# Raw weights loaded by pairs of units, and a written-out order for the first batch, in an attention and two-layer expert kernel on one core

## The chip, the cores and the metric

The kernel runs on one NeuronCore of a Trainium2 chip. The metric is the device time of one execution in microseconds (us); smaller is better. Beside an execution's own time stands its span, from the first to the last instruction that the hardware profiler recorded. The engines are TensorE (PE: matmuls; PEld: its weight loads), VectorE (DVE), ScalarE (ACT), GpSimd (POOL) and SyncE (SP, which here only issues DMAs). Each engine works through its own instructions in the order in which they stand, and semaphores tie the engines together.

## The reference

Four batches, eight heads, 576 tokens, head size 64; q, k and v arrive as 32-bit floats, the weights as 64-bit floats (read by the kernel as 16-bit pieces).

```python
q_d, k_d, v_d = means of 4 consecutive tokens            # 144 of them
out_up = repeat(softmax(q_d k_d^T / 8) v_d, 4)           # coarse attention, spread back to 576 tokens
out_local = softmax(mask(|i - j| < 4, q k^T / 8)) v      # 7 neighbours of each token
x = (out_up + out_local) as [2304 tokens, 512]
x = (silu(x @ w_gate) * (x @ w_val)) @ w_out             # 512 -> 1536 -> 512
h = x @ w_in
out = (h * clip(h + 3, 0, 6) / 6) @ w_out2               # 512 -> 2048 -> 512
```

## The kernel before

The 2304 tokens are cut into five blocks (`BLOCKS`, up to 512 tokens). Each block runs 68 **units** of the two layers, of five kinds: G (gate), V (value), O (first output), H (second input), P (second output). Units come in pairs, and a unit is 12 matmuls of 512 columns in block 0: each weight and each activation is held as a high and a low part of a reduced 32-bit format, and three products of parts are summed (`HIGH`, `LOW`). A unit's product (`pG`, `pV`, `pH`) takes one of two PSUM banks `mm`; a V unit's product can start only when the bank of the G unit before it has been read by ScalarE (`sl`, L962).

Weights of block 0 go through a chain. `load_unit` (L196, SP's queue) fetches a raw unit, 512 KB of 64-bit numbers, into one of four buffers; `decode_a` (L216, ACT, `top`) and `decode_b` (L225, DVE, `w`) make 32-bit numbers of it and set the buffer free; `split_unit` makes the high part on ACT (L238, `wr`) and the low part on DVE (L239, `wr`) for a pair; the pair is also written to DRAM (`kept`, ACT's queue), from where the blocks after it read it. `prefetch(i)` runs, for unit i of the loop, the load of unit i+8, `decode_a` of i+5, `decode_b` of i+4 and the split of i+3. The next SP load in line waits until the `decode_b` of four units earlier is done.

Ahead of the units stands **the front**, `first_batch`: batch 0's attention on TensorE, in five tiles of 122 tokens (the last has 88). `load_T` turns q and k; `down_scores`, `down_trans`, `down_values` do the coarse attention by head pairs c = 0 to 3. For a tile i, `scores(i)` makes the products (`fS`), the row maxima (DVE, `fnm`) and eight exponentials (ACT, `held`); `norm(i)` divides (DVE, `fsm`, `held`); `trans(i)` turns the result (`fPT`), whose first half ACT and second half DVE copy (`turned`); `values(i)` makes the output (`fO`), and `put_cols` writes its high part on ACT (L275) and its low part on DVE (L276) into `xr`, the units' input. `fill` (L469) puts products that nothing reads ahead of a turning, `FILL_P[i]` of them.

A scheduler orders the instructions of an engine, except those passed through `keep_in_program_order` (`together`, `behind`, `late`), which keep the order of the program among themselves. In the front TensorE's instructions are so pinned, and the decodes and splits (`behind`), but not the front's own DVE and ACT instructions.

Of the kernel before, what the change touches and what calls it, by code (L numbers as in the profile page):

```python
# [21 lines left out]
P = 128  # L22
# [10 lines left out]
HALVES = 1  # L33
# [10 lines left out]
FILL_P = (4, 8, 8, 8, 8)  # L44
# [3 lines left out]
def tile_kernel(  # L48
# [86 lines left out]

    def behind(ins):

        if front[0]:
            tc.keep_in_program_order(ins)
# [26 lines left out]
    def view(t, i):  # L166
        return t[:, i % 2, :].rearrange("p (c e) -> p c e", c=NC)

# [8 lines left out]
    def load_unit(i):  # L177
# [12 lines left out]
        if kind in "GVH":  # L190
            src = src[:, f * P * m:(f + 1) * P * m].rearrange("(c p) f -> p c f", p=P)
        else:
            src = src[f * P:(f + 1) * P, :].rearrange("p (c e) -> p c e", c=NC)
        if wide:
            raw[i] = sp.tile([P, 4 * DM + 32], I16, tag="w64", name=f"w64_{i}", bufs=4)
            behind(nc.sync.dma_start(raw[i][:, 1:1 + 4 * DM].rearrange("p (c e) -> p c e", c=NC), src))  # L196
        else:
            nc.sync.dma_start(view(w32[i // 2], i), src)
# [34 lines left out]
    def split_unit(i):  # L233
        if i % 2:
            return
        s = w32[i // 2].rearrange("p u (c e) -> p u c e", c=NC)
# [33 lines left out]
    def put_cols(bi, col, xv):  # L270
# [4 lines left out]
        nc.scalar.activation(dst[:, :, 0], xv, AF.Copy)  # L275
        nc.vector.tensor_tensor(dst[:, :, 1], xv, dst[:, :, 0].bitcast(F32), op=ALU.subtract)  # L276
# [39 lines left out]


    def first_batch():
# [6 lines left out]
        with tc.tile_pool(name="fp", bufs=1) as fp:  # L325
# [125 lines left out]
            for base, sgn in ((-UPAD, -1), (UPAD + 3, 1)):  # L451
# [3 lines left out]
                )  # L455
            kT = fp.tile([P, NC, S + 6], F32, name="fkT")
            nc.vector.memset(kT[:, :, :3], 0.0)
            nc.vector.memset(kT[:, :, S + 3:], 0.0)
# [12 lines left out]
            def load_T(w, c):  # L471
                src = qn[w, c // 2]
                for th in range(2):
# [13 lines left out]
                    if w == "q":  # L487
                        nc.vector.tensor_scalar(dst, ps[:, :, :TT], 0.125, None, op0=ALU.mult)
                        nc.scalar.activation(small, ps[:, :, TT:], AF.Copy, scale=1 / 128)
                    else:  # L490
                        nc.scalar.activation(dst, ps[:, :, :TT], AF.Copy)
                        nc.vector.tensor_copy(small, ps[:, :, TT:])
# [7 lines left out]
            def down_scores(c):  # L500
# [14 lines left out]
                for par in range(2):  # L515
                    nc.vector.tensor_reduce(nm[:, par], pss[par], axis=AX.X, op=ALU.max, negate=True)
                    for half in range(2):
                        nc.scalar.activation(
# [6 lines left out]
            def down_trans(c):  # L525
                pd = dst[c]
                for par in range(2):
# [3 lines left out]
                    nc.scalar.activation(dpt[h], pt, AF.Copy)  # L531
# [625 lines left out]
```

## Time and profile before

| | |
|---|---|
| time, median of 3 runs (lowest to highest) | 967.41 us (967.27 to 970.9) |
| profiled execution: its own time; its span | 967.38 us; 965.7 us |
| busy: PE, PEld, DVE, ACT, POOL (share of the span) | 948.1 (98%), 803.2 (83%), 724.6 (75%), 501.6 (52%), 110.4 (11%) us |
| mean granted TensorE clock, as a share of the full one | 0.993 |
| the front, first turned q to the start of the units proper | 6.83 to 64.11 us |

The own time is 1.68 us more than the span, and within 0.03 us of the median. Matmuls are pipelined and their ends are modelled, so a PE that is shown as busy may still be waiting; a stretch of matmuls is best timed from the start of one row to the start of the next. DMA shares are of 16 engines, and can exceed 1 where transfers of several queues overlap.

### The profile page before, as it was taken

To read this page: it belongs to the slowest core of one execution; us is meant where nothing else is said; L and a number is where in the kernel's file an instruction comes from. 1 tells how busy PE (TensorE), PEld (TensorE's weight loads), DVE (VectorE), ACT (ScalarE), POOL (GpSimd) and SP (SyncE) were. 2 spreads that over 40 slices of the span, in tenths; PEclk is the share of its full clock that TensorE was granted. 3 is DMA by queue.
4 is the path that set the end of the run, shared out by engine and by line. 5 is a ranking of instruction groups with operands and counts; after the bars stand their busy time and mean duration, and the time that the engine had idled before them with its cause. 6 is when DMAs were issued, how large, how long until landed. Compare 5 with 4: busy or idle time off the path is not lost.

```text
span 965.7 us, 13166 instructions
## 1 busy us (share of the span) xinstructions
PE 948.1 (98%) x4928; PEld 803.2 (83%) x4928; DVE 724.6 (75%) x1059; ACT 501.6 (52%) x928; POOL 110.4 (11%) x125
## 2 busy tenths in 40 slices
PE   9899999999999999999999999999999999999997
PEld 7687888777899988878888778888888788999996
DVE  4678976899979979999774799997337994445652
ACT  4666566876543567553333764443335445444542
POOL 7610002200062300014320000000000000000000
PEclk9999999999999999999999999999999999999999
DMA  8999799866799823359972222462322323443331
GB/s 195 228 270 340 247 366 311 183 198 236 261 246 264 166 86 109 99 188 242 199 157 88 88 67 67 173 216 90 97 100 93 103 88 108 154 131 130 120 122 33
DMA packets 116340, 160.80 MB, mean 167 GB/s; under 512 B 61868, under 2 KB 83756, under 8 KB 116276
## 3 DMA queue, kind: packets, MB, share of 16 engines
q1 hardware_dynamic: 67892, 131.41, 42.7%
q0 software_dynamic: 43488, 10.72, 11.1%
q10 hardware_dynamic: 4896, 17.83, 4.7%
q8 instruction: 39, 0.64, 0.3%
q14 instruction: 25, 0.20, 0.1%
HBM read 137.29 MB, written 22.54 MB: 166 GB/s over the span
## 4 chain that ended last, share of the span: by engine, by line
PE 78%; DVE 7%; DMA 1%; ACT 1%; issue 1%; ACTq 0%; DVEq 0%
PE pH L956 19%; PE aP L998 18%; PE aO L998 13%; PE pV L956 13%; PE pG L956 12%; DVE wr L239 2%; PE pS L881 1%; PE pO L731 1%; DMA w<-in_moe_w_out_dram 1%; DVE xf L856 1%; PE pPT L724 1%; PE px L847 1%; DMA w<-in_moe_w_gate_dram 1%; DVE pv L827 1%; DVE w L225 1%
## 5 line engine op out<-in xcount | busy, mean ns | idle before, releaser
L239 DVE TENSOR_TENSOR wr<-w,wr 128x1024 fp32r<-128x1024 f32 x170 | 207.8, 1222 | 123.8 <-ACT wr L238 123.6
L238 ACT ACTIVATE wr<-w 128x1024 fp32r<-128x1024 f32 x170 | 179.5, 1056 | 119.1 <-issue 57.7
L956 PE MATMUL pH<-x,wr 128*128 128x512 f32 (+1 forms) x960 | 212.2, 372 | 0.0
L998 PE MATMUL aP<-wr,gH 128*128 128x512 f32 x864 | 211.4, 395 | 0.3 <-ACT gH L973 0.3
L956 PEld LDWEIGHTS pH<-x,wr 128*128 128x128 f32 x960 | 173.1, 188 | 25.3 <-issue 2.9
L998 PEld LDWEIGHTS aP<-wr,gH 128*128 128x128 f32 x864 | 159.8, 188 | 34.8 <-issue 2.5
L956 PE MATMUL pG<-xr,wr 128*128 128x512 f32 (+3 forms) x732 | 156.4, 369 | 1.0 <-DVE sl L968 0.6
L956 PE MATMUL pV<-xr,wr 128*128 128x512 f32 (+1 forms) x720 | 153.9, 369 | 0.9 <-ACT sl L962 0.9
L998 PE MATMUL aO<-gV,wr 128*128 128x512 f32 (+1 forms) x720 | 154.4, 371 | 0.0
L956 PEld LDWEIGHTS pG<-xr,wr 128*128 128x128 f32 x732 | 133.3, 191 | 18.5 <-DVE sl L968 1.0
L998 PEld LDWEIGHTS aO<-gV,wr 128*128 128x128 f32 x720 | 132.4, 190 | 16.9 <-DVE gV L974 0.2
L956 PEld LDWEIGHTS pV<-xr,wr 128*128 128x128 f32 x720 | 130.8, 188 | 18.4 <-ACT sl L962 1.8
L971 ACT ACTIVATE h<-pH,consts 128x512 f32<-128x512 f32 (+1 forms) x80 | 51.4, 643 | 59.7 <-PE pH L956 59.5
L973 ACT ACTIVATE gV<-sl 128x512 fp32r<-128x512 f32 (+1 forms) x60 | 35.0, 584 | 85.5 <-DVE sl L968 85.2
L216 ACT ACTIVATE top<-w 128x512 f16<-128x512 bf16 x68 | 52.3, 790 | 22.9 <-DMA w<-in_moe_w_out_dram 7.7
L962 ACT ACTIVATE sl<-pG 128x512 f32<-128x512 f32 (+1 forms) x60 | 33.0, 551 | 59.6 <-PE pG L956 57.0
L973 ACT ACTIVATE gH<-h 128x512 fp32r<-128x512 f32 (+1 forms) x80 | 46.9, 586 | 31.9 <-DVE h L972 31.6
L972 DVE SCALAR_TENSOR_TENSOR h<-h,pH 128x512 f32<-128x512 f32 (+1 forms) x80 | 50.5, 632 | 15.6 <-ACT h L971 15.1
L790 DVE TENSOR_TENSOR pr<-q,k 128x1792 f32<-128x1792 f32 x27 | 54.6, 2021 | 9.4 <-DMA k<-in_k_dram 9.2
L974 DVE TENSOR_TENSOR gH<-h,gH 128x512 fp32r<-128x512 f32 (+1 forms) x80 | 50.6, 633 | 10.9 <-ACT gH L973 10.5
L827 DVE TENSOR_TENSOR pv<-sc,v 128x1792 f32<-128x1792 f32 x27 | 54.6, 2022 | 0.5
L793 DVE TENSOR_REDUCE sc<-pr 128x28 f32<-128x1792 f32 x27 | 54.4, 2015 | 0.1
(131 smaller groups left out, 761.9 us busy)
## 6 DMA issues: line engine op xcount, KB each, us to landing
w<-kept SPq DMA_DIRECT2D x136, 512.0 KB
kept<-w ACTq DMA_DIRECT2D x34, 512.0 KB
w<-in_moe_w_out_dram SPq DMA_DIRECT2D x28, 512.0 KB
w<-in_moe_w_in_dram SPq DMA_DIRECT2D x16, 512.0 KB
w<-in_moe_w_gate_dram SPq DMA_DIRECT2D x12, 512.0 KB
w<-in_moe_w_val_dram SPq DMA_DIRECT2D x12, 512.0 KB
out_dram<-os SPq DMA_DIRECT2D x16, 256.0 KB
dnq<-in_q_dram POOLq DMA_DIRECT2D x24, 144.0 KB, 7.8
```

Of the source, the lines that this page charges most:

```text
L216: behind(nc.scalar.activation(halves(top[i % 2], 2, F16)[:, :, 1], h3.bitcast(BF16), AF.Copy))
L238: behind(nc.scalar.activation(r[:, :, 0], s, AF.Copy))
L239: behind(nc.vector.tensor_tensor(r[:, :, 1], s, r[:, :, 0].bitcast(F32), op=ALU.subtract))
L790: nc.vector.tensor_tensor(pr, qt[:, a:a + SUB, None, :].to_broadcast([P, SUB, W, D]), win(kt, a, SUB), op=ALU.mult)
L793: nc.vector.tensor_reduce(sc[:, a:a + SUB], pr, axis=AX.X, op=ALU.add)
L827: nc.vector.tensor_tensor(pr, pe[:, a:a + SUB, :, None].to_broadcast([P, SUB, W, D]), win(vt, a, SUB), op=ALU.mult)
L956: nc.tensor.matmul(ps[:, cs], r[:, a, c], x[:, c, b_, cs], start=part is HIGH and a == c == 0, stop=part is LOW and c == NC - 1,)
L971: nc.scalar.activation(h, ps, AF.Relu, scale=1 / 6, bias=half1[:, 0:1])
L972: nc.vector.scalar_tensor_tensor(h, h, 1.0, ps, op0=ALU.min, op1=ALU.mult)
L973: nc.scalar.activation(g[:, 0, :nt], h, AF.Copy)
L974: nc.vector.tensor_tensor(g[:, 1, :nt], h, g[:, 0, :nt].bitcast(F32), op=ALU.subtract)
L998: nc.tensor.matmul(ps, **one, start=f_ == 0 and a == b_ == 0, stop=f_ == nf - 1 and b_ == 1,)
```

## The change

1. **Loads by pairs.** A raw load of a G, V or H unit no longer fetches 128 columns of all 512 rows, but 256 columns (both units of the pair) of half the rows: the same 512 KB, in rows twice as long. `split_unit` works on the pair as one flat row of 1024 and hands out the units as views. O and P loads keep their shape.
2. **Orders in the front.** DVE's and ACT's instructions of the front are all pinned (`Ordered`, and `behind` in `put_cols`). `scores` loses its exponentials to a new function `weights`, and the program is written anew with `scores` of a later tile ahead of `trans` of an earlier one. The decodes and splits of the first four units of the loop stay pinned too (`EARLY_W`).
3. **Fills**: 16 in place of 36.
4. **Units 0 and 1 begun in the front**: `begin_unit` multiplies the first 244 columns of unit 0 ahead of `trans(3)` and the first 366 of unit 1 ahead of `trans(4)`, and `run_unit` does the rest (268 and 146). Before, unit 0 alone was cut, 244 and 268.

```diff
-HALVES = 1
+HALVES = 2
-FILL_P = (4, 8, 8, 8, 8)
+EARLY_W = 4
+FILL_P = (4, 4, 4, 4, 0)
...
+    class Ordered:
+        def __init__(self, engine):
+            self.engine = engine
+        def __getattr__(self, name):
+            op = getattr(self.engine, name)
+            def issue(*args, **kw):
+                tc.keep_in_program_order(op(*args, **kw))
+            return issue
...
-            src = src[:, f * P * m:(f + 1) * P * m].rearrange("(c p) f -> p c f", p=P)
+            h = i % 2
+            src = src[h * DM // 2:(h + 1) * DM // 2, (f - h) * P * m:(f - h + 2) * P * m]
+            src = src.rearrange("(c p) f -> p c f", p=P)
...
-        behind(nc.scalar.activation(r[:, :, 0], s, AF.Copy))
-        behind(nc.vector.tensor_tensor(r[:, :, 1], s, r[:, :, 0].bitcast(F32), op=ALU.subtract))
+        r = r.rearrange("p a u c e -> p a (u c e)")
+        behind(nc.scalar.activation(r[:, 0], s, AF.Copy))
+        behind(nc.vector.tensor_tensor(r[:, 1], s, r[:, 0].bitcast(F32), op=ALU.subtract))
+        by = "p a (c u e) -> p u a c e" if units[i][0] in "GVH" else "p a (u c e) -> p u a c e"
+        r = r.rearrange(by, u=2, c=NC)
...
+    def begin_unit(i, n):
+        kind, f, bi = units[i]
+        ps = bank("mm", f"p{kind}{bi}_{f}", 2)
+        products(ps, split[i], xr[bi], slice(0, n), tc.keep_in_program_order)
+        begun[i] = ps, n
...
+            vec, act = Ordered(nc.vector), Ordered(nc.scalar)
...
             scores(0)
             ahead = down_sums(1, ["qk"], first_max[0])
+            weights(0)
             down_trans(2)
             down_scores(3)
             scores(1)
+            weights(1)
             next(ahead)
             next(ahead)
+            norm(0)
             down_values(0)
             down_values(1)
-            norm(0)
+            scores(2)
             trans(0)
+            down_trans(3)
+            prefetch(3 - LR)
+            weights(2)
             prefetch(4 - LR)
-            down_trans(3)
-            down_values(2)
-            norm(1)
-            scores(2)
-            down_values(3)
-            prefetch(5 - LR)
-            values(0)
             for i in range(1, NT):
...
-                trans(i)
+                norm(i)
                 if i + 2 < NT:
                     scores(i + 2)
                 if i == 1:
-                    prefetch(6 - LR)
+                    down_values(2)
+                    down_values(3)
+                values(i - 1)
+                if i >= NT - HALVES:
+                    begin_unit(i - NT + HALVES, (i - 1) * QT)
+                trans(i)
+                if i + 2 < NT:
+                    weights(i + 2)
+                    prefetch(4 + i - LR)
                 if i == 2:
                     prefetch(7 - LR)
-                if i + 1 < NT:
-                    norm(i + 1)
                 next(ahead, None)
-                values(i)
+            values(NT - 1)
-        front[0] = False
...
+            front[0] = i < EARLY_W
             prefetch(i)
```

How the instructions stand on the engines, before and after. First TensorE, behind `down_values(0)` and `(1)` (`fdO`), before: the fills and the turning of tile 0 (`fPT`), then `down_trans(3)` (`fdT`), `down_values(2)`, `scores(2)` (`fS`, its weight loads left out), `down_values(3)`, and only then `values(0)` (`fO`).

```order
L469 MATMUL fPT_0_561<-ident 128x256
...
L620 MATMUL fPT_0_561<-ident,held 128x122 x4
L620 MATMUL fPT_1_571<-ident,held 128x122 x4
L724 MATMUL fdT_582<-ident,fdpd_492 72x72 x4
...
L538 MATMUL fdO_596<-fvd,fdpT_476 72x65 x2
...
L572 MATMUL fS_0_614<-band,pick 122x512
...
L538 MATMUL fdO_638<-fvd,fdpT_587 72x65 x2
...
L638 MATMUL fO_658<-tmp 128x122
```

The same place after:

```order
L607 MATMUL fS_0_560<-band,pick 122x512
...
L503 MATMUL fPT_0_576<-ident 128x256
...
L660 MATMUL fPT_0_576<-ident,held 128x122 x4
L660 MATMUL fPT_1_586<-ident,held 128x122 x4
L766 MATMUL fdT_592<-ident,fdpd_489 72x72 x4
...
L607 MATMUL fS_0_631<-band,pick 122x512
...
L572 MATMUL fdO_647<-fvd,fdpT_473 72x65 x2
...
L572 MATMUL fdO_660<-fvd,fdpT_597 72x65 x2
...
L678 MATMUL fO_673<-tmp 128x122
```

`scores(2)` now stands ahead of the turning of tile 0, and `scores(3)` ahead of `down_values(2)` and `(3)`; both `down_values` stand directly ahead of `values(0)`.

Second VectorE, around the low part of the first weight pair (L239 before, L252 after; `L145` is the line of `Ordered`). Before, with the division of tile 2 (`fsm`, `held`) ahead of it:

```order
L225 SCALAR_TENSOR_TENSOR w_0_580<-w_1_257,top_161 128x512
L599 TENSOR_SCALAR fsm_612<-fsm_612 122x8
L600 RECIPROCAL fsm_612<-fsm_612 122x8
L601 TENSOR_TENSOR held<-held,fsm_612 122x1024
L239 TENSOR_TENSOR wr_655<-w_0_580,wr_655 128x2x512
L276 TENSOR_TENSOR xr_671<-fO_658,xr_671 128x4x122
L625 COPY turned<-fPT_1_692 128x488
```

After:

```order
L291 TENSOR_TENSOR xr_686<-fO_673,xr_686 128x4x122
L145 COPY turned<-fPT_1_699 128x488
L237 SCALAR_TENSOR_TENSOR w_0_620<-w_1_257,top_161 128x512
L252 TENSOR_TENSOR wr_717<-w_0_620,wr_717 128x1024
L145 TENSOR_SCALAR fsm_558<-fsm_558 122x8
L145 RECIPROCAL fsm_558<-fsm_558 122x8
L145 TENSOR_TENSOR held<-held,fsm_558 122x1024
L145 TENSOR_REDUCE fnm_730<-fS_0_731 88x4
```

The low part moved from behind the division of tile 2 to ahead of it.

Third ScalarE, from the output of tile 2 to the first `sl`. Before:

```order
L275 ACTIVATE xr_671<-fO_808 128x4x122
L627 ACTIVATE turned<-fPT_0_827 128x488
L216 ACTIVATE top_161<-w_5_651 128x512
L238 ACTIVATE wr_912<-w_2_727 128x2x512
L231 DMA kept_126<-w_2_727 128x1024
L275 ACTIVATE xr_671<-fO_850 128x4x122
L216 ACTIVATE top_159<-w_6_724 128x512
...
L238 ACTIVATE wr_954<-w_4_910 128x2x512
...
L216 ACTIVATE top_159<-w_8_907 128x512
...
L962 ACT_TABLE_LOAD
L962 ACTIVATE sl_0_946<-pG_0_921 128x512
```

After:

```order
L290 ACTIVATE xr_686<-fO_800 128x4x122
L243 DMA kept_126<-w_2_789 128x1024
L145 ACTIVATE turned<-fPT_0_832 128x488
L290 ACTIVATE xr_686<-fO_851 128x4x122
L145 ACTIVATE turned<-fPT_0_879 94x4x88
L290 ACTIVATE xr_686<-fO_891 128x4x24
L290 ACTIVATE xr_906<-fO_891 128x4x64
L228 ACTIVATE top_161<-w_5_713 128x512
L251 ACTIVATE wr_918<-w_2_789 128x1024
L995 ACT_TABLE_LOAD
L995 ACTIVATE sl_0_939<-pG_0_819 128x512
L228 ACTIVATE top_159<-w_6_786 128x512
```

The second pair's split and the decodes of units 5 and later moved from among the front's tiles to behind its last output. From the end of block 0 on the PE order is the same in both.

## Rows read from the trace of the kernel before

**Rows 1.** A late stretch: length; busy us (instructions) by engine; clock, DMA share, GB/s.

```profile
600.00:800.00 200.00, 199.46 (x884) 163.71 (x883) 154.56 (x202) 84.31 (x116) 0.00 (x0) 1.00 0.35 117
```

**Rows 2.** The chain that ended last: shares of the span by engine.

```profile
PE 78%; DVE 7%; DMA 1%; ACT 1%; issue 1%; ACTq 0%; DVEq 0%
```

**Rows 3.** Timeline of PE in the front: start, length, line, what, [idle before it, releaser].

```profile
23.75 0.60 PE L572 MATMUL fS<-band,pick 64*122 64x512 bf16 x4
...
25.16 1.25 PE L538 MATMUL fdO<-fvd,fdpT 72*72 72x65 f32 x16
26.63 1.25 PE L538 MATMUL fdO<-fvd,fdpT 72*72 72x65 f32 x16 [0.22 <-ACT fdpT L531]
...
30.08 0.75 PE L724 MATMUL fdT<-ident,fdpd 72*72 72x72 f32 x8 [0.92 <-DVE tmp L545]
33.03 1.57 PE L538 MATMUL fdO<-fvd,fdpT 72*72 72x65 f32 x16 [2.21 <-ACT fdpT L531]
...
37.24 1.25 PE L538 MATMUL fdO<-fvd,fdpT 72*72 72x65 f32 x16
...
41.37 1.05 PE L469 MATMUL fPT<-ident 128*128 128x256 bf16 x8
42.26 1.00 PE L620 MATMUL fPT<-ident,held 122*128 122x122 f32 x8
...
64.11 6.95 PE L956 MATMUL pG<-xr,wr 128*128 128x244 f32 x32
...
71.12 5.74 PE L956 MATMUL pV<-xr,wr 128*128 128x512 f32 x24
```

**Rows 4.** Timeline of PE behind the front.

```profile
80.49 3.03 PE L956 MATMUL pG<-xr,wr 128*128 128x512 f32 x12 [0.57 <-DVE sl L968]
...
95.76 5.60 PE L956 MATMUL pG<-xr,wr 128*128 128x512 f32 x24
101.20 5.60 PE L956 MATMUL pV<-xr,wr 128*128 128x512 f32 x24
```

**Rows 5.** Two single microseconds; columns as in rows 1.

```profile
34.00:35.00 1.00, 1.00 (x8) 0.70 (x8) 0.32 (x2) 0.00 (x0) 0.40 (x2) 0.50 1.30 254
...
65.00:66.00 1.00, 1.00 (x7) 1.00 (x6) 0.54 (x1) 1.00 (x3) 0.00 (x0) 0.50 1.02 373
```

**Rows 6.** Timeline of ACT in the front and at its end.

```profile
23.41 0.37 ACT L588 ACTIVATE held<-fS,fnm 122x128 f32<-122x128 f32 x1
...
26.16 0.42 ACT L531 ACTIVATE fdpT<-fdT 72x288 f32<-72x288 f32 x1
...
40.82 0.81 ACT L216 ACTIVATE top<-w 128x512 f16<-128x512 bf16 x1
41.46 1.08 ACT L238 ACTIVATE wr<-w 128x1024 fp32r<-128x1024 f32 x1
42.39 0.61 ACT L275 ACTIVATE xr<-fO 128x488 fp32r<-128x488 f32 x1
...
68.08 1.28 ACT L962 ACT_TABLE_LOAD   x1 [1.06 <-DVE w L225]
```

**Rows 7.** Timeline of DVE in the front.

```profile
26.34 0.17 DVE L599 TENSOR_SCALAR fsm<-fsm 122x8 f32<-122x8 f32 x1 [1.57 <-ACT held L588]
...
27.93 1.28 DVE L586 TENSOR_REDUCE fnm<-fS 122x4 f32<-122x512 f32 x2
...
38.55 0.15 DVE L543 TENSOR_SCALAR fdsd<-fdO 72x4 f32<-72x4 f32 x1
...
39.28 0.68 DVE L225 SCALAR_TENSOR_TENSOR w<-w,top 128x512 int32<-128x512 int32 x1
...
42.76 1.22 DVE L239 TENSOR_TENSOR wr<-w,wr 128x1024 fp32r<-128x1024 f32 x1
```

**Rows 8.** Unit 9's raw load: its issue on SP's queue, and its `decode_a` on ACT.

```profile
60.70 0.36 SPq L196 DMA_DIRECT2D w<-in_moe_w_out_dram  x1
...
71.03 0.79 ACT L216 ACTIVATE top<-w 128x512 f16<-128x512 bf16 x1 [1.06 <-DMA w<-in_moe_w_out_dram]
```

More of the change, by code (lines that the diff above doesn't have):

```diff
@@ L315, in down_T, with products @@
             yield
+    HIGH, LOW = ((0, 0), (1, 0)), ((0, 1),)
+    begun = {}
+    def products(ps, r, x, cs, pin=lambda ins: None):
+        for part in (HIGH, LOW):
+            for c in range(NC):
+                for a, b_ in part:
+                    pin(nc.tensor.matmul(
+                        ps[:, cs], r[:, a, c], x[:, c, b_, cs],
+                        start=part is HIGH and a == c == 0, stop=part is LOW and c == NC - 1,
+                    ))
+    def begin_unit(i, n):
[3 more added lines that the diff above has]
+        begun[i] = ps, n
     def first_batch():
@@ L554, in first_batch @@
             first_max = []
+            scored = {}
             def scores(i):
@@ L584, in scores, with weights @@
                 for par in range(2):
-                    ps = pss[par][:n, :, :w_]
-                    nc.vector.tensor_reduce(nm[:n, :, par], ps, axis=AX.X, op=ALU.max, negate=True)
-                    for c in range(NC):
-                        nc.scalar.activation(
-                            p_[:n, c, par, :w_], ps[:, c], AF.Exp, bias=nm[:n, c, par:par + 1],
-                            accum_out=sm[:n, c, par:par + 1],
-                        )
+                    vec.tensor_reduce(nm[:n, :, par], pss[par][:n, :, :w_], axis=AX.X, op=ALU.max, negate=True)
                 pe[i], tot[i] = p_, sm
+                scored[i] = pss, nm
                 if i == 0:
                     first_max.append(nm[:n, 0, :1])
+            def weights(i):
+                n = size(i)
+                pss, nm = scored.pop(i)
+                for par in range(2):
+                    for c in range(NC):
+                        act.activation(
+                            pe[i][:n, c, par, :n + 6], pss[par][:n, c, :n + 6], AF.Exp,
+                            bias=nm[:n, c, par:par + 1], accum_out=tot[i][:n, c, par:par + 1],
+                        )
             def norm(i):
@@ L937, in tile_kernel @@
     state = {}
-    HIGH, LOW = ((0, 0), (1, 0)), ((0, 1),)
     def run_unit(i):
@@ L946, in run_unit @@
         if kind in "GVH":
-            ps = bank("mm", f"p{kind}{bi}_{f}", 2)[:, :nt]
+            ps, done = begun.pop(i, (None, 0))
+            if ps is None:
+                ps = bank("mm", f"p{kind}{bi}_{f}", 2)
             x = xr[bi] if kind != "H" else state["x2"]
-            cols = [slice(0, nt)]
-            if i < HALVES:
-                cols = [slice(0, 244), slice(244, nt)]
-            for cs in cols:
-                for part in (HIGH, LOW):
-                    for c in range(NC):
-                        for a, b_ in part:
-                            nc.tensor.matmul(
-                                ps[:, cs], r[:, a, c], x[:, c, b_, cs],
-                                start=part is HIGH and a == c == 0, stop=part is LOW and c == NC - 1,
-                            )
+            products(ps, r, x, slice(done, nt))
+            ps = ps[:, :nt]
             if kind == "G":
```

50 lines of the change are left out of this document (23 added, 27 removed).

## The prediction

> **What bounds the kernel now.** I read the chain that ended last, then the busy times by stretch, then the timeline of each engine in the first 100 us. The chain is 78% PE [rows 2], and a late stretch of 200 us has PE busy for 199.46, at full clock, with the DMA engines at 0.35 [rows 1]. So from the second block on only TensorE's work counts, and that work and its order are the same after the change. What can move is the beginning, and what it gains or loses there stays to the end as long as nothing else becomes late.
>
> In the front, the reader is to see three losses. PE waits 0.22, 0.92 and 2.21 us between 26.4 and 33.0 [rows 3], 3.35 us in all. Behind these waits the granted clock is at 0.50, its lower level of 1.2 GHz [rows 5]: the stretch from 33.03 to 37.24 holds one `down_values` and one `scores`, which at full clock take 1.25 and, from 23.75 to 25.16, 1.41 [rows 3]; 4.21 less 2.66 is 1.55 us. And the clock is at 0.50 again at 65 us [rows 5], with PE busy in every row before it: 32 matmuls from 64.11 to 71.12, 8 of 244 columns, 12 of 268 and 12 of 512, are 11,312 columns, and by the 24 of 512 that take 5.74 us [rows 3] they would need 5.3; 7.01 less 0.2 of small matmuls is 6.8, so 1.5 us went.
>
> Behind the front, the eight units from 71.12 to 95.76 take 24.64 us [rows 3, 4]. A pair takes 5.44 us (95.76 to 101.20) [rows 4], four pairs 21.8, and four small turnings some 0.9, which leaves 2.0 us of waits; one of them shows as 0.57 on DVE's `sl` [rows 4].
>
> **The change, part by part.**
>
> *Loads by pairs.* Bytes and the count of DMAs stay, rows are twice as long. In the front no decode waits for a load; behind it some do, as `decode_a` of unit 9 by 1.06 us [rows 8]. None of the waits of PE in rows 3 and 4 names a DMA. Bounds: nothing, up to that 1.06 per late load where ACT's wait holds up `sl`. I take nothing; the cover is the lead of the loads over the units, and what happens if it is gone is the third rival. The split writes the same 1024 elements in one run: ACT and DVE have slack, nothing.
>
> *Fills.* 20 fewer. Eight take 0.89 us (41.37 to 42.26) [rows 3], so 2.2 us of PE's work goes, but only where PE is what is late.
>
> *Units begun in the front.* 24 products more in number, of the same columns in sum except that unit 1 is cut in two: 12 more products. Between nothing (by columns) and 12 times the 0.11 of a fill, 1.3 us; I take 0.3, since 146 columns are near the size of a fill.
>
> *Orders.* Here a walk is needed: each engine in its new order, with the durations of before, an instruction starting when its engine is free and what it reads is there. Durations: eight exponentials 2.75 us (23.41 to 26.16) [rows 6]; a decode on ACT 0.64, a split on ACT 0.93 with 1.08 to its end [rows 6]; a `norm` 1.59 (26.34 to 27.93), a row-maximum pair 1.28, a DVE decode 0.68, what follows a `down_values` 0.73 (38.55 to 39.28), a split on DVE 1.22 [rows 7]; a `values` about 3.0 (37.24 to 41.37, less a `down_values`) [rows 3].
> - The copies behind `down_trans(2)` now stand behind all eight exponentials of tile 0. The bank that `down_values(0)` needs is free at 26.6 in place of 25.2: PE waits 1.4, and `down_values(1)` ends at 28.8.
> - `scores(2)` to 30.2, fills and `trans(0)` to 31.6, `down_trans(3)` 32.2, `scores(3)` 33.6, both `down_values` 35.9, with no wait. The waits of 0.92 and 2.21 are gone.
> - DVE is late next: it holds `decode_b(0)` for ACT's `decode_a(0)` (after the exponentials of tile 1, at 33.5), then `norm(1)` to 35.7, maxima of tile 3 to 37.0, and only then frees the bank of `down_values(2)`, at 37.8. PE waits 2.0 us, and `values(0)` runs from 37.9 to 40.9; before, from 38.3 to 41.4. `scores(3)`, 1.4 us of PE, is done already.
> - ACT then has `xr` of tile 0, half of `turned` of tile 1 to 42.4, exponentials of tile 3 to 45.1, a decode to 45.8, the first split to 46.9. DVE stands at its half of that split from 43 to 47.0, and behind it is queued `norm(2)`, which ends at 49.8. PE, done with `scores(4)` and `values(1)` at 46.5, waits 3.2 us for it: `trans(2)` starts at 49.85, where before it started at 48.6.
> - `values(2)` 51.0 to 55.0, 244 columns of unit 0 to 56.3, `trans(3)` to 57.7, `values(3)` to 60.95, 366 columns of unit 1 to 62.8, `trans(4)`, `values(4)` to 66.4, the rests of both units from 66.75 to 69.0.
> - The second pair's split and the table load (1.28) [rows 6] now follow the last `xr` on ACT: split to 68.6, table to 69.85, `sl` to 70.4, and the first V product starts at 70.45. Before, 71.12: at full clock throughout, 0.67 us are won.
>
> So 3.35 us of waits are replaced by 1.4, 2.0, 3.2 and 1.25. From 70.45 on, the same walk gives eight units without a wait (DVE's `sl`, splits and decodes come 0.5 to 1 us ahead of their need): 2.0 won.
>
> *The clock.* The last stretch before the units is like that of before (small products, and the last four fills gone). A lower level there would stretch 4,968 columns, 2.3 us, to 4.6, but ACT hides 1.25 of it: between 0 and 1.1 lost, I take 0.5. For the wait of 3.2 us at 46.5 the nearest row is the lower level at 34 us, behind 0.92 and 2.21 [rows 3, 5]: a stretch like that costs 1.55 us, here in full, since `values(2)` and what follows it are PE's. I take one such stretch, 1.6.
>
> Sum: -0.67 - 2.0 + 0.5 + 1.6 = -0.57 us, against the profiled execution's own 967.38: **966.8 us**. That execution is 0.03 us from the median of the runs. The case's own range: 965 to 968.5.
>
> **The rivals.**
>
> *The clock does not fall behind the 3.2 us wait.* For it: `values(1)` and `scores(4)` keep PE busy up to 46.5, where in rows 3 only 0.75 us of work lay between the two waits of before. Against it: at 64 us the level fell with no wait shown at all [rows 5]. Without the 1.6 the sum is -2.2, 965.2 us; without the 0.5 too, 964.7. The Trainium skill (TensorE: Matmul & The Clock Gate, HAM oscillation) lays the fall to long idle gaps between groups of matmuls, and a single gap like this one would not bring it; by it the time would be this rival's 965.2. The row at 65 us, low with PE busy, does not agree with idle gaps as the only cause, so I give this rival less.
>
> *The walk's waits don't come.* If DVE and ACT meet their places earlier than walked, PE's work alone counts: fills 2.2, waits 3.35, low clock 3.05, waits behind the front 2.0, less 0.3 for cut products: 10.3, so 957.1 us at the very best; half of it, 962.2. For it: PE is the chain's engine [rows 2]. Against it: the pinned order puts a DVE split behind eight exponentials, which no duration here undoes. It passes 0.5% (4.84 us) only if nearly half of all that can be won is.
>
> *Slower: the raw loads lose their lead.* Unit 9's load went out at 60.70, among the front's tiles, and was decoded at 71.03 [rows 8], 10.3 us later. Now it goes behind `decode_b(5)`, which stands behind the last output of the front, at 70. With loads of 10 us in a ring of four, unit 16's `decode_a` comes at 103, ahead of `sl` of unit 13's gate on ACT, and PE, which wants that bank at 101.8, waits some 3 us; each further round of four units, 10.3 plus 1.8 of decoding against 10.9 of PE, adds 1.2, up to five rounds: 3 to 9 us, 970 to 976. It decides if loads still take 10 us past 92 us. Against it: the 10.3 us were taken while the two chunks of q, k and v were moved too, and longer rows may shorten them.
>
> *Two more stretches at the lower clock*, behind the 2.0 us wait at 36 too: another 1.6, 968.4.
>
> **How the numbers follow.** Forecast, 966.8: 0.45. No fall in the middle, 964.7 to 965.2: 0.22. Waits that don't come, 957 to 963: 0.13, nearly all of it past 0.5%. Two low stretches, 968 to 970: 0.10. Loads late, 970 to 976: 0.10, most of it under the bound of 972.2. Half a per cent, 4.84 us, is about what a measurement of this kernel can tell from no change. So faster by over 0.5% 0.12, within it 0.81, slower 0.07. The range leaves out half of each far rival: 962.0 to 971.0.
>
> **What would show it.** Right: `values(0)` starts near 38, DVE sits idle for 3 to 4 us ahead of its first split, `trans(2)` starts near 50, the first V product at 70 to 72, and `pG` of units 10 and 11 near 93 to 95 in place of 95.76. Wrong: no idle time of DVE at that split, or a first V product before 68 (the walk is too slow); ACT waiting for DMAs ahead of `sl` between 90 and 130 with PE idle (the slower rival); a clock of 1.00 from 46 to 56 (no fall).

## The result, and the profile after

The changed kernel takes 979.11 us in the median of four runs (972.28 to 982.27), against 967.34 for the kernel before in the same series: 1.0111 times as long, 95% interval 1.0075 to 1.0146. The forecast was 966.8 us with a range up to 971.0; the time is above the range, and slower by more than half a per cent.

The four runs differ among themselves by 10 us, and their mean granted clocks differ with them (0.993, 0.988, 0.988, 0.983). Span times (1 - clock) is an estimate of what the lower level cost a run; it holds if PE was what was late meanwhile. It is 6.8, 11.7, 11.7 and 16.7 us, and without it the four runs stand at 965.5 to 968.9. This **time at full clock**, and the **clock loss** beside it, are used for all kernels below, with two warnings. First, the clock is also low at the end of every profile, behind PE's last product (before: from 962.1 us to the end at 965.7, the last product having ended at 958.8); that part, 0.7 to 2.6 us of each profile's clock loss, costs nothing. Second, other kernels' runs are brought together less well: over the 105 runs of the kernel before that were taken beside the experiments, the standard deviation falls from 3.0 to 2.3 us only, and between runs of one kernel, over 256 runs, a microsecond of clock loss goes with some 0.75 us of time. So differences of less than some 3 us in that column show little. For these 105 runs the medians of the four series are 960.1 to 961.9 us at full clock, and the mean clock losses 6.7 to 9.1 us. So the change lost some 5 us at full clock and some 4 us more of clock; with four runs of the change, these do not add up exactly to the 11.8 between the medians.

The profiled execution is the fastest of the four: its own time is 972.28, its span 970.5. Three stretches from its table of windows (columns as in rows 1), answering to [rows 1, 5], and its chain, answering to [rows 2]:

```profile
38.00:39.00 1.00, 0.84 (x4) 0.66 (x6) 0.68 (x4) 0.00 (x0) 1.00 (x2) 0.50 1.48 175
47.00:48.00 1.00, 1.00 (x16) 0.89 (x12) 0.40 (x1) 1.00 (x7) 1.00 (x2) 0.50 1.27 109
65.00:66.00 1.00, 1.00 (x8) 1.00 (x7) 0.32 (x1) 0.00 (x0) 0.00 (x0) 1.00 0.00 0
600.00:800.00 200.00, 199.41 (x885) 163.61 (x884) 155.14 (x205) 84.34 (x117) 0.00 (x0) 1.00 0.34 117
```

```profile
PE 66%; DVE 16%; DMA 8%; issue 5%; ACT 3%; POOL 0%; SPq 0%; DVEq 0%; ACTq 0%; POOLq 0%
```

The late stretch is as before. But DVE and DMA have taken 16% and 8% of the chain, where they had 7% and 1%; and the clock is at 0.50 from 38 to 48 us, one stretch of 10 us, and no longer at 65. The timeline of PE, answering to [rows 3, 4], and below it DVE's at 257 us and SP's queue at the raw loads of units 8 and 9, answering to [rows 8]:

```profile
27.03 2.26 PE L572 MATMUL fdO<-fvd,fdpT 72*72 72x65 f32 x32 [1.50 <-ACT fdpT L145]
...
38.16 0.76 PE L678 MATMUL fO<-tmp 72*128 72x122 f32 x2 [1.87 <-DVE fdsd L145]
...
43.44 1.04 PE L503 MATMUL fPT<-ident 128*128 128x256 bf16 x4
...
46.03 0.85 PE L607 MATMUL fS<-band,pick 64*88 64x376 bf16 x4
...
48.07 0.48 PE L678 MATMUL fO<-tmp 72*128 72x122 f32 x2
...
53.14 1.05 PE L660 MATMUL fPT<-ident,held 122*128 122x122 f32 x8 [1.37 <-DVE held L145]
...
74.16 1.20 PE L340 MATMUL pV<-xr,wr 128*128 128x512 f32 x4 [0.95 <-ACT sl L995]
...
98.16 1.07 PE L340 MATMUL pG<-xr,wr 128*128 128x512 f32 x4
...
192.29 0.71 PE L773 MATMUL pO<-pT,dnv 72*64 72x144 f32 x6 [1.56 <-DMA dnv<-in_v_dram]
...
260.08 0.41 PE L889 MATMUL px<-ident,o 128*128 128x128 f32 x2 [1.96 <-DVE o L875]
```

```profile
257.77 0.69 DVE L237 SCALAR_TENSOR_TENSOR w<-w,top 128x512 int32<-128x512 int32 x1 [2.02 <-DMA kept<-w]
258.38 1.22 DVE L252 TENSOR_TENSOR wr<-w,wr 128x1024 fp32r<-128x1024 f32 x1
259.52 0.42 DVE L875 TENSOR_TENSOR o<-pv 128x256 f32<-128x256 f32 x1
```

```profile
71.74 0.35 SPq L208 DMA_DIRECT2D w<-in_moe_w_out_dram  x1
...
74.13 0.33 SPq L208 DMA_DIRECT2D w<-in_moe_w_out_dram  x1
```

Read against [rows 3, 4], the starts of the same instructions give the place of the loss in this execution: the first V product is 3.04 us late (74.16, was 71.12), unit 10 is 2.40 late (98.16, was 95.76), the first G product of block 1 is 5.51 late (272.40 against 266.89 in the two timelines), and the end 4.8. So 3 us went in the front and 3 us in block 0 behind unit 10 (0.7 came back later, where the trace of before has a stretch at 0.50 near 345 us that this one has not). In block 0 PE now waits 1.56 for `dnv` (the sums of v of the next batch, for the coarse attention) and 1.96 for `o` (DVE's attention of the units ahead). The last comes of the order on DVE: it stands 2.02 us at a decode whose buffer is still being written out to `kept`, and `o` is queued behind it.

### The profile page after: what moved, and what is told of

It is laid out like the page before. It is cut to its first block, busy times and chain, and to the rows that moved or that the text cites. A ratio compares the mean times of both kernels' runs of the same rounds, so it can differ in the third digit from the quotient of the medians.

```text
span 970.5 us, 13153 instructions
## 1 busy us (share of the span) xinstructions
PE 947.2 (98%) x4920; PEld 801.0 (83%) x4920; DVE 724.3 (75%) x1059; ACT 502.1 (52%) x928; POOL 110.5 (11%) x125
## 3 DMA queue, kind: packets, MB, share of 16 engines
q0 software_dynamic: 43488, 10.72, 11.1%
## 4 chain that ended last, share of the span: by engine, by line
PE 66%; DVE 16%; DMA 8%; issue 5%; ACT 3%; POOL 0%; SPq 0%; DVEq 0%; ACTq 0%; POOLq 0%
PE aP L1031 14%; PE pH L340 14%; PE aO L1031 10%; PE pG L340 10%; PE pV L340 10%; DVE wr L252 4%; DMA k<-in_k_dram 3%; DVE w L237 2%; DVE pv L869 2%; DMA w<-in_moe_w_val_dram 2%; DMA dnv<-in_v_dram 2%; DVE xf L898 1%; DVE h L1005 1%; DVE sc L835 1%; DVE pr L832 1%
## 5 line engine op out<-in xcount | busy, mean ns | idle before, releaser
L252 DVE TENSOR_TENSOR wr<-w,wr 128x1024 fp32r<-128x1024 f32 x170 | 207.5, 1221 | 123.7 <-ACT wr L251 123.4
L340 PE MATMUL pG<-xr,wr 128*128 128x512 f32 (+5 forms) x744 | 155.4, 363 | 2.1 <-DVE sl L1001 1.3
L832 DVE TENSOR_TENSOR pr<-q,k 128x1792 f32<-128x1792 f32 x27 | 54.5, 2020 | 11.4 <-DMA k<-in_k_dram 11.2
```

The costliest lines, as they stand in the source:

```text
L252: behind(nc.vector.tensor_tensor(r[:, 1], s, r[:, 0].bitcast(F32), op=ALU.subtract))
L340: pin(nc.tensor.matmul(ps[:, cs], r[:, a, c], x[:, c, b_, cs], start=part is HIGH and a == c == 0, stop=part is LOW and c == NC - 1,))
L832: nc.vector.tensor_tensor(pr, qt[:, a:a + SUB, None, :].to_broadcast([P, SUB, W, D]), win(kt, a, SUB), op=ALU.mult)
```

## The experiments

Three theories were put against each other. **A**: the front's order lets the clock fall for longer. **B**: the decodes and splits of the loop's first four units, pinned behind the front, come late, and what follows from them too. **C**: the longer rows delay other transfers. Every kernel ran beside the kernel before, those with one letter in one series; the table has all of them.

| run | median us | ratio to before, 95% interval | clock loss, mean | at full clock, median |
|---|---|---|---|---|
| the change | 979.11 | 1.0111 (1.0075 to 1.0146) | 11.7 | 965.7 |
| e1_pairs_only | 966.51 | 0.9989 (0.9953 to 1.0024) | 8.0 | 960.6 |
| e2_fills_back | 981.38 | 1.0125 (1.0081 to 1.0168) | 14.2 | 967.4 |
| e3_loop_free | 975.23 | 1.0056 (1.0029 to 1.0083) | 13.9 | 961.6 |
| e4_before_few | 967.76 | 0.9964 (0.9936 to 0.9992) | 8.2 | 958.7 |
| f1_before_pinned | 977.67 | 1.0087 (1.0056 to 1.0117) | 11.4 | 966.2 |
| f2_waits_filled | 979.44 | 1.0101 (1.0074 to 1.0128) | 8.8 | 970.3 |
| f3_behind_norms | 971.24 | 1.0019 (0.9997 to 1.0041) | 6.8 | 964.9 |
| f4_pairs_filled | 964.40 | 0.9947 (0.9926 to 0.9967) | 4.1 | 959.9 |
| g1_after_hand | 974.25 | 1.0066 (1.0036 to 1.0096) | 11.1 | 964.0 |
| g2_norms_hand | 970.84 | 1.0015 (0.9990 to 1.0040) | 6.5 | 963.6 |
| g3_norms_free | 969.46 | 1.0014 (0.9988 to 1.0041) | 9.0 | 960.7 |
| g4_norms_sums25 | 965.02 | 0.9966 (0.9943 to 0.9989) | 3.6 | 961.5 |
| h1_dve_backlog | 977.89 | 1.0110 (1.0069 to 1.0152) | 10.6 | 967.6 |
| h2_act_backlog | 971.35 | 1.0038 (1.0015 to 1.0062) | 6.6 | 964.9 |
| h3_best_sums25 | 962.49 | 0.9959 (0.9930 to 0.9987) | 3.4 | 960.2 |

**e1_pairs_only.** The kernel before, with the edits of `load_unit` and `split_unit` from the diff and nothing else of it.

> The kernel before with only the loads of the raw weights changed (pairs, half the row chunks each, and the flat split). Three theories of the 11.7 us that the change lost. A, the front's new orders with fewer fills leave TensorE's clock at its lower level longer, and differently from run to run. B, the pinned decodes and splits of units 4 to 7 hold back the raw loads of units 8 and on (unit 8's went out at 71.74 in place of 58.61), which shows as waits of some 3.8 us in block 0's second half. C, the longer rows themselves delay something, for instance the table or down-path transfers beside them. By A and B this kernel runs like before: 965 to 969 us, ratio 0.998 to 1.002, raw load of unit 8 issued near 59 us. By C it is slower by 3 us or more, 970.5 us and up, with PE waiting in block 0's second half for what a DMA brings.

No difference from before can be told: C falls, and the loads by pairs are worth nothing that these runs can tell, as forecast.

**e2_fills_back.** The changed kernel.

```diff
-FILL_P = (4, 4, 4, 4, 0)
+FILL_P = (4, 8, 8, 8, 8)
```

> The changed kernel with the fill products of before (4, 8, 8, 8, 8 a turning in place of 4, 4, 4, 4, 0): 20 more, some 2.2 us of TensorE's work, put between a turning's two halves. A (clock): granted clock behind 38 us higher, the low stretch of 10 us shorter, and the median 3 to 10 us below that of the changed kernel, 969 to 976 us. B (lead) and C (rows): nothing won, between 0 and +2.2 us where TensorE is what is late, 977 to 982 us.

Nothing won. The 1.7 us more at full clock are near the 2.2 of the fills, but too few to tell from nothing. The fills stand behind the waits or between the halves of a turning; with a clock loss of 14.2 they do not hold the clock there. In this form A falls.

**e3_loop_free.** The changed kernel.

```diff
-EARLY_W = 4
+EARLY_W = 0
```

> The changed kernel with the loop's decodes and splits (units 4 to 7 ahead) no longer pinned behind the front: the scheduler places them as in the kernel before. B (lead): unit 8's raw load goes out before 65 us in place of 71.74, the waits of 1.56 and 1.96 us in block 0's second half fall under 1 us in sum, and the time is 3 to 4 us below that of the changed kernel at the same clock. A: no change beyond what the clock of single runs does, within 2 us at equal clock. C: the same as A.

B holds: 4.1 us less at full clock, and in the profile PE waits 0.52 for `dnv` and 0.65 for `o`. The new front itself is then worth no more than the old one, 961.6 against 960.1 in its series. But the clock loss is still 13.9, and the first V product comes at 80.42: the scheduler sets decodes ahead of copies that PE waits for, as in its row at 63.83 (timeline of PE):

```profile
63.83 0.43 PE L684 MATMUL fO<-turned,vw 128*64 128x122 f32 x4 [2.02 <-ACT turned L145]
```

**e4_before_few.** The kernel before.

```diff
-FILL_P = (4, 8, 8, 8, 8)
+FILL_P = (4, 4, 4, 4, 0)
```

> The kernel before with the fewer fills of the change (4, 4, 4, 4, 0) and nothing else of it. A, if the fills alone carry the clock: slower than before by 2 us or more, with low clock over more than the 7 us of the profile of before. A, if it is the long waits of the new order that bring the low clock: within 1 us of before, or up to 2.2 us faster. B and C: also within 1 us of before or up to 2.2 us faster.

The clock loss is that of before, so fewer fills alone don't bring more of it. The ratio is clear of 1; 1.4 us less at full clock fit the 2.2 that the 20 fills are worth by their length, but are too few to tell the size.

**f1_before_pinned.** The kernel before, with the loop's line of the change.

```diff
-        front[0] = False
...
+            front[0] = i < EARLY_W
             prefetch(i)
```

> The kernel before, with one thing of the change: the loop's decodes and splits that are issued by units 0 to 3 (those of units 3 to 8 ahead) stay in program order behind the front. B (lost lead, from the other side): the raw load of unit 8 goes out near 70 us in place of 58.6, and the time at equal clock is 3 to 6 us above that of before, whose median at full clock is some 960.5 us (time less span times (1 - clock)); so some 964 to 967 at full clock, with the wait for DVE's o near 256 us that the changed kernel has. If the pinning costs only together with the new front: within 1 us of before at equal clock.

B holds from the other side too: 966.2 at full clock, 4.3 us above the 961.9 of before in its series, with the old front. The clock loss rises too, to 11.4 where before has 7.4 in this series, so the clock is not the front's alone: in the profile it is at 0.50 for 3.4 us each from 72.1 and from 195.0, at the first two of these waits. The third, for `o`, is the changed kernel's (timeline of PE):

```profile
72.18 1.22 PE L956 MATMUL pV<-xr,wr 128*128 128x512 f32 x2 [2.03 <-ACT sl L962]
...
193.91 0.71 PE L731 MATMUL pO<-pT,dnv 72*64 72x144 f32 x6 [1.61 <-DMA dnv<-in_v_dram]
...
263.83 0.41 PE L847 MATMUL px<-ident,o 128*128 128x128 f32 x2 [2.15 <-DVE o L833]
```

Unit 8's load went out at 66.74 (58.61 before). And DVE, which had 35.01 us of work between 20 and 70, has 30.15 here and 27.54 in the changed kernel (tables of windows of the three, in this order):

```profile
20.00:70.00 50.00, 46.61 (x436) 38.11 (x436) 35.01 (x67) 33.57 (x119) 23.27 (x21) 0.93 1.13 241
```

```profile
20.00:70.00 50.00, 46.61 (x446) 37.85 (x444) 30.15 (x62) 30.55 (x116) 23.44 (x21) 0.97 0.98 190
```

```profile
20.00:70.00 50.00, 44.80 (x409) 35.42 (x409) 27.54 (x58) 27.36 (x111) 22.82 (x20) 0.90 0.91 174
```

**f2_waits_filled.** The changed kernel; `spare_cols` are columns of a bank that `down_scores(3)` leaves free.

```diff
+            fill_cols(spare_cols[0], 13, 512 - 2 * NJ)
             down_values(0)
...
+                if i == 1:
+                    fill(bank("acc2", "wfill"), 17)
                 values(i - 1)
...
-FILL_P = (4, 4, 4, 4, 0)
+FILL_P = (4, 4, 16, 4, 0)
```

> The changed kernel with fill products in its three waits of the front: 13 ahead of down_values(0), 17 ahead of values(0), 12 more ahead of trans(2). They write PSUM columns that nothing reads. A, if idle time of TensorE lets its clock fall: granted clock 0.995 or more in most runs, no stretch of 10 us at 0.50 behind 38 us, 966 to 970 us. If it is the small products of the front and not the idle time: clock as in the changed kernel (0.983 to 0.993), 977 to 981 us.

A poor instrument. The first fills themselves waited 2.24 us, for ACT's exponentials (`fdpd`) that read the bank whose spare columns they write, and so brought a wait of their own, longer than the 1.50 that they were to fill. In the profile no stretch at 0.50 is left in the front, but the runs' clock loss of 8.8 is not clearly under 11.7 (six and four runs), and some 5 us more were lost at full clock; in the profile the wait for `dnv` is 4.53, where the changed kernel's was 1.56. Inconclusive.

**f3_behind_norms.** The changed kernel; `prefetch` leaves out these two calls.

```diff
                 norm(i)
+                if i == 2:
+                    split_unit(0)
...
                     down_values(3)
+                    decode_b(0)
```

> The changed kernel with two of DVE's instructions moved in its pinned order: decode_b(0) from ahead of norm(1) to behind down_values(3), and the first split from ahead of norm(2) to behind it. By the walk of the prediction the waits of 1.87 ahead of values(0) and 1.37 ahead of trans(2) fall under 0.6 each, and trans(2) starts 2 us or more earlier than at 53.14. A (idle time sets the clock): also fewer low stretches, 3 to 8 us in all, 971 to 976 us. If waits of this size have nothing to do with the clock: 2 to 3 us, 975 to 977 us, mean clock as in the changed kernel. If the order of these two instructions costs nothing: no change, 978 to 981 us.

The wait ahead of `values(0)` fell to 0.20, `trans(2)` starts at 45.78 without one (0.62 are left ahead of `trans(3)`), the first V product came at 67.41, 6.75 us earlier, and the clock loss is 6.8. That is as A expects when the waits become shorter: 8 us faster than the change, most of it by the clock loss. But the profile shows where the front's gain went, a wait of 6.87 us (timeline of PE):

```profile
67.41 1.43 PE L340 MATMUL pV<-xr,wr 128*128 128x512 f32 x5 [0.95 <-ACT sl L998]
...
191.65 1.23 PE L776 MATMUL pO<-pT,dnv 72*64 72x144 f32 x6 [6.87 <-DMA dnv<-in_v_dram]
```

PE meets `dnv` at the same 192 us as in the changed kernel, however early it comes.

**f4_pairs_filled.** The kernel before with pair loads, `FILL_P` as in the change, and fills in the two waits of [rows 3].

```diff
+            fill(bank("acc0", "wfill0"), 8)
             down_trans(3)
+            fill(bank("acc1", "wfill1"), 20)
             down_values(2)
```

> The kernel before with pair loads, the fewer fills of the change ahead of the turnings, and 8 and 20 fills in the waits of 0.92 and 2.21 us at 29 and 31 us instead. A (idle time sets the clock): no stretch at 0.50 near 34 us, the clock at 0.995 or more in most runs, 960 to 964 us. If the small products set it: as the kernel before with fewer fills, 965 to 969 us.

The clearest run for A: the same order as e1, with PE working through the two waits, and the clock loss is 4.1 in place of 8.0 (clocks of 0.990 to 0.999 against 0.984 to 0.997). The fewer fills ahead of the turnings, the other difference from e1, did not lower it in e4 (8.2). Its row for the front, and PE there:

```profile
20.00:70.00 50.00, 49.22 (x464) 39.81 (x464) 36.45 (x67) 36.46 (x123) 24.50 (x22) 1.00 1.17 271
```

```profile
28.32 1.04 PE L474 MATMUL wfill<-ident 128*128 128x256 bf16 x8
29.40 0.75 PE L731 MATMUL fdT<-ident,fdpd 72*72 72x72 f32 x8
29.99 2.35 PE L474 MATMUL wfill<-ident 128*128 128x256 bf16 x20
```

At 1.00 throughout, the first V product comes at 65.64. This kernel beats both.

**g1_after_hand, g2_norms_hand.** The changed kernel, and f3, with part of the loop's work set into DVE's and ACT's gaps of the front.

```diff
                 norm(i)
+                if i == 4:
+                    decode_b(4)
+                    load_raw(8)
...
                 trans(i)
+                if i == 3:
+                    decode_a(5)
+                if i == 4:
+                    decode_a(6)
+                    decode_b(5)
+                    load_raw(9)
```

> The changed kernel, still with the loop's work pinned behind the front, but with the decodes of units 4 and 5 and the raw loads of units 8 and 9 placed by hand into idle gaps of the front (last decode_b(5) before the end of the front). B (the raw loads' lead is what the pinning costs): unit 8's load issued 8 us or more earlier than at 71.74, the waits for dnv (1.56 at 192) and o (1.96 at 260) under 1.5 us in sum, and time at full clock some 962 to 963.5 in place of 966.5; with the clock as it was, 973 to 976 us. If the lead of these loads is not it: full-clock time 965 or more, 977 to 980 us.

> The changed kernel with both mends: decode_b(0) and the first split behind the norms (as in f3_behind_norms) and the decodes of units 4 and 5 and the loads of units 8 and 9 by hand in the front. If A and B are both causes and add: the front ends as in f3 (first V product at 66 to 68 us), block 1 starts at 268 us or before in place of 273.2, time at full clock 958 to 961, and 963 to 967 us with the clock loss of 6.8 that f3 had. If the front's gain is taken by something else (dnv must wait for the same transfers anyway): 969 to 972 us as f3.

Unit 8's load goes out at 63.29 in g1, 8.5 us earlier than in the change, and the time at full clock is 1.7 us lower, 1.3 in g2: too little to tell from nothing. The waits stay: 4.17 for `dnv` and 0.79 and 2.14 for `o` in g1. Two loads' lead is not what was lost: of g1's expectation by B the median came true, but neither the waits nor the time at full clock, and of g2's neither time did.

**g3_norms_free.** f3 with `EARLY_W = 0`.

> The changed kernel with decode_b(0) and the first split behind the norms, and the loop's work not pinned. B: the waits for o at 260 us gone and dnv's under 2 us, full-clock time 957 to 961; but the scheduler sets decodes ahead of the copies that PE waits for in the front (as in e3_loop_free, 2.02 us ahead of values(3)), so the first V product comes 1 to 4 us later than in f3. In sum 964 to 969 us. If the pinning was not the cause: 970 to 973 us.

At full clock 960.7, 4 us under f3: B. No wait for `dnv`, 0.64 for `o`; the front pays with a wait of 2.97 us in `values(3)`, and the clock loss is 9.0. With both mends, f3's and the free loop, the new front is level with the kernel before (1.0014), so as far as these runs can tell, these two parts of the change hold the whole loss.

**g4_norms_sums25.** f3, with the sums of v begun earlier.

```diff
-SUMV = 31
+SUMV = 25
```

> f3_behind_norms with the sums of v for the down path begun behind unit 25 in place of 31 (some 15 us earlier); the loop's work stays pinned. If the wait of 6.87 us for dnv at 191.65 was the start of that chain: it falls under 1 us and block 1 starts 4 to 7 us earlier than at 273.2, 965 to 968 us. If late raw loads and their decodes set block 0's second half whatever dnv does: the wait turns up elsewhere (for o, or for kept copies), block 1 starts within 2 us of 273, 969 to 972 us.

No wait for `dnv` is left, block 1 starts at 264.07 in place of 273.23, and the median is 6 us lower, 3.4 of it at full clock and 3.2 in the clock loss: in f3's profile the clock is at 0.50 from 188.5 to 195.3, at the wait that is gone here. `o` is waited for as in all pinned kernels:

```profile
250.17 0.41 PE L892 MATMUL px<-ident,o 128*128 128x128 f32 x2 [2.08 <-DVE o L878]
```

**h1_dve_backlog, h2_act_backlog.** The kernel before, with work that nothing uses right behind the front's last output, on DVE (7.0 us) or on ACT (3.7 us).

```diff
             prefetch(i)
+            if i < 4:
+                tc.keep_in_program_order(nc.vector.tensor_reduce(
+                    scr[:, :3], xr[0][:, :3, 1, :].bitcast(F32), axis=AX.X, op=ALU.max))
```

> The kernel before, with four row-maxima of 1536 columns (some 1.7 us each, 6.9 in sum, by the 1.28 of two of 512) that nothing uses on DVE, right behind the front's last output; decodes and raw loads of units 4 to 7 stay free. It puts on DVE about what pinning moved behind the front (DVE busy 35.0 of the 50 us from 20 to 70 before, 30.2 when pinned), and leaves the loads nearly where they were (unit 8's near 59 us). If the backlog of DVE's work is what the pinning costs: the waits for o near 236 and 252 grow to 2 us or more in sum and the time at full clock rises by 3 to 6 us, 971 to 975 us. If it is the late raw loads: within 1.5 us of before at full clock.

> The same on ACT: sixteen small copies (some 0.25 us each, 4 in sum) behind the front's last output, about what pinning moved there (ACT busy 33.6 of 50 us before, 30.6 when pinned). If ACT's backlog is what the pinning costs, by a late sl, decode or split: 3 to 6 us at full clock. If not: within 1.5 us of before, as the slack of ACT, 17 to 20 busy of each 30 us behind the front, takes it.

DVE's pile brings what pinning brings, and more: 6.4 us at full clock, a clock loss of 10.6 (before: 6.7 in this series), and waits for `o` (timeline of PE):

```profile
250.65 0.41 PE L848 MATMUL px<-ident,o 128*128 128x128 f32 x2 [1.30 <-DVE o L834]
...
267.26 0.41 PE L848 MATMUL px<-ident,o 128*128 128x128 f32 x2 [2.35 <-DVE o L834]
```

It leaves the first raw loads their lead (SP's queue at unit 8's load, DVE at the first row-maximum, PE at the first V product):

```profile
66.17 0.35 SPq L197 DMA_DIRECT2D w<-in_moe_w_out_dram  x1
...
72.36 1.75 DVE L1093 TENSOR_REDUCE scr<-xr 128x3 f32<-128x1536 f32 x1
...
78.71 1.63 PE L957 MATMUL pV<-xr,wr 128*128 128x512 f32 x6
```

The front ran 7.6 us late in this execution (the first V product of before came at 71.12). Unit 8's load goes out 12.5 us ahead of that product, as before (58.61), and ahead of the whole pile; the next two keep their lead within 0.7 us, and only the four behind them come late, by 2.6 to 5.3 us when the front's lateness is taken off.

ACT's pile costs 3.7 us at full clock, the size that its expectation names for a backlog that counts. It comes by other waits: `sl` by 1.32 at 75, 2.04 at 319 and 1.19 at 446; `o` is waited for 0.41 as before, with unit 8's load on time at 58.59. Pinning moved about as much of ACT's work behind the front (33.57 to 30.55 us busy from 20 to 70), so a part of its cost may be ACT's.

**h3_best_sums25.** f4 with `SUMV = 25`.

> f4_pairs_filled with the sums of v begun behind unit 25 in place of 31, as in g4_norms_sums25. If the start of that chain sets its end: the wait of 0.92 for dnv at 183.6 goes, and with it the stretch of lower clock that such waits bring in some runs: 962 to 964 us. If the chain's end is set by transfers that it shares the DMA engines with: no change, 964 to 966 us.

The wait for `dnv` is gone, and 962.49 us is the lowest median of all; by their intervals, f4 and h3 can't be told apart. The clock loss is 3.4, low as in f4.

## Why the prediction was wrong, point by point

**The walk of the front held.** Walked waits of 1.4, 2.0, 3.2 and 1.25 us stand in the profile as 1.50, 1.87, 1.37 and 0.95; the third is shorter because the low clock had delayed PE by then: `trans(2)` starts at 53.14, and DVE stood idle 2.88 us ahead of its first split, walked 3 to 4. If the whole lateness of `trans(2)` is the clock's, 3.3 us (53.14 less the walked 49.85), the first V product would come at 70.9 with full clock, an estimate; walked was 70.45.

**The term of the clock failed.** The step was: one stretch like that of [rows 3, 5] behind the wait of 3.2, 1.6 us, and 0.5 for the end. It came behind the wait of 1.87 already, and it lasted 10 us, through `values(0)`, `trans(1)` and `scores(4)` (38.16 to 48.07, 9.91 us; in the timeline of before one `values` takes 3.04, four fills 0.45, one `trans` 0.93 and the last `scores` 1.09, 5.51 in sum): 4.4 us, 3.3 of them, by the estimate above, not made good by the wait that follows. Nor had the sum a term for stretches elsewhere, which come and go from run to run. The clock loss is 3 to 16 us (clocks of 0.997 to 0.984) in the kernel before, and the change moved its mean from some 7.7 to 11.7 (four runs; e2, e3 and g1, with the same waits in the front, have 11.1 to 14.2); the sum had it fall, from before's 1.55 and 1.5 in the front to 1.6 and 0.5. The profiled execution of the change has the least loss of its four runs, 6.8, so it does not show where the others lost more. The rival on the other side, that the clock would not fall at all, was further off still.

What sets it is shown in part. Filling two waits of 0.92 and 2.21 us halved the loss (f4 against e1), shortening two waits took 5 us of it (f3 against the change), removing one of 6.87 at 191 us another 3.2 (g4 against f3), and fills that do not stand in waits did nothing (e2, e4). So idle time of PE, even 1 to 2 us at a time, brings the lower level about here, but not each time: in the 17 profiles, from 10 us on, it began in or within 2.5 us behind 12 of the 52 waits of 1 to 2 us, and 17 of the 23 longer ones. One wait of 1.7 us for `o` near 345 us stands in 16 profiles, and the level fell behind it in that of before alone. And seven stretches near the end of the front, the one at 65 us of [rows 5] among them, have no wait of over 0.35 us close ahead; they are not explained. The Trainium skill (TensorE: Matmul & The Clock Gate, HAM oscillation) lays the oscillation to idle gaps between groups of matmuls. These runs agree in the main, but for those seven. The prediction read from it that a single gap of 3.2 us would not bring the level down, and a gap of 1.87 us did.

**"2.0 won behind the front" was 0.6.** From the first V product to unit 10 it takes 24.00 us, before 24.64. The 2.0 was a remainder; PE's timeline of before shows waits of 0.57 and 0.54 in that stretch and no more. One of 0.76 at 83.7 remains, and one of 0.95 for `sl` stands ahead of the first V product.

**The pinned loop was costed at nothing in the sum, and cost some 4 us** at full clock (e3, f1 and g3, with it taken out, put in and taken out). This is the step that failed with the clock: "from the second block on only TensorE's work counts [...] as long as nothing else becomes late". It was read from 600 to 800 us; nearer the front, the trace of before itself has PE wait for `o`, with the lower level behind it (timeline of PE; one microsecond, columns as in rows 1):

```profile
343.66 0.41 PE L847 MATMUL px<-ident,o 128*128 128x128 f32 x2 [1.70 <-DVE o L833]
...
345.00:346.00 1.00, 1.00 (x5) 1.00 (x4) 0.94 (x4) 0.32 (x1) 0.00 (x0) 0.50 0.40 86
```

The third rival had the cause, the pinning of the decodes, with 0.10, and in its 3 to 9 us a size that holds some 4. Its mechanism was wrong: it had ACT wait for raw loads from 90 us on and so hold up `sl`. ACT's waits for raw loads from 60 to 130 us fell, from 11.9 us in sum to 6.3, and `sl` of unit 13 does not keep PE waiting at 102; the price comes due at 192 (`dnv`) and 260 (`o`), some 120 and 190 us later. And of its 0.10 most was to lie under 972.2, while 0.07 was put on slower; the two do not fit together.

Between these ends the chain is shown in part. All eight pinned kernels (the change, e2, f1 to f3, g1, g2, g4) have 1.79 us or more of waits for `o` in block 0, the seven with a free loop and no pile (the kernel before, e1, e3, e4, f4, g3, h3) at most 0.65. A pile on DVE alone brings such waits (h1), one on ACT does not (h2). For `dnv`, an earlier start of the chain removes the wait (g4).

For `o` the traces show one link more. In the nine kernels with the wait, h1 among them, DVE comes to the last `o` of block 0 by decode (`w`), sum (`pv`), decode, split (`wr`), and that last decode waits 1.86 to 2.19 us for a write to `kept` (the rows at 257.77 above). In the other eight DVE comes to it by split, sum, decode, and no row of DVE in block 0 waits for `kept`. Before (timeline of DVE):

```profile
249.18 1.22 DVE L239 TENSOR_TENSOR wr<-w,wr 128x1024 fp32r<-128x1024 f32 x1
250.31 0.69 DVE L832 TENSOR_TENSOR pv<-pv 128x512 f32<-128x512 f32 x1
250.91 0.69 DVE L225 SCALAR_TENSOR_TENSOR w<-w,top 128x512 int32<-128x512 int32 x1
251.52 0.42 DVE L833 TENSOR_TENSOR o<-pv 128x256 f32<-128x256 f32 x1
```

So the wait goes with another order of DVE's instructions 190 us behind the pin, and that order is the scheduler's, settled before the run. It is a rival to B's "come late" that no run here tests: how much of the 2 us is the order's, and how much is lateness of the decodes and their `kept` writes, stays open, and so does why a pin or a pile near 70 us changes the order there. Unit 8's lead is not the link: it was there in h1, and in g1 but for some 2 us, and the waits stayed.

**Right as forecast**: loads by pairs nothing (e1), the 2.2 us of 20 fills as far as these runs can tell (1.4 less in e4, 1.7 more in e2), and the work from block 1 on unchanged (698.1 us to the end of the span, before 698.8 with the stretch near 345 us).

## What to carry to other kernels

Where the clock's loss differs by several us from run to run, look at time and clock of every run; a single trace shows one draw of it. A wait of 1 to 2 us on TensorE can cost more than its length, and useless products set exactly into it, on a bank that is already free, can be the cheapest cure. And pinning optional work behind a stage takes it out of that stage's gaps: ask which engine must do it later, compare the order of the engines' instructions far behind the stage as well, and look for the bill there, not just behind the stage.

## What was not expected of the hardware

Some waits of 1.5 to 2.2 us were followed by stretches at the lower level that were several times as long, with PE busy through most of each: from 28.0 to 31.5 us in f3, 37.8 to 48.0 in the changed kernel, 32.2 to 49.2 in e4. Most waits of 1 to 2 us were followed by none. And executions of one kernel on one chip differed by 11 us (964.41 to 975.92 for the kernel before beside e1 to e4), with clocks from 0.997 to 0.984.
